# Weight differences of MoE 2 made during MoE 1, new planner durations, and routing ahead in VectorE's order

## The chip, the cores and the metric

One Trainium2 chip, of which the kernel uses one core. The time is device microseconds of one execution; three executions of the kernel before took 1979.09, 1979.22 and 1980.27 us (median 1979.22). All arithmetic is in 32-bit floats; matrix products are made from pairs of a rounded high part and a low part (three products instead of one).

## The reference

Three stages follow each other:

- Attention over a packed set: for 4 batches x 8 heads, 32 pack queries attend over 576 keys and values of 64 elements, and the 576 queries attend over the 32 results. Output: 2304 tokens x 512.
- MoE 1: h = x w_in (512 x 2048), g = h * clip(h + 3, 0, 6) / 6, y = g w_out (2048 x 512).
- MoE 2: a gate (512 x 8), exp of the logits, eight rounds in which P is divided by its row sums, then by its column sums, and scaled by N/E; then for each of 8 experts relu(x w1[e]) w2[e] with 1024 hidden columns, weighted by P[:, e] and summed.

## The kernel before

The 2304 tokens are 6 blocks of 384. Hidden columns are taken in groups of 256: MoE 1 has 8 groups, MoE 2 has 4 per expert, 32 in all.

The program isn't written in its final order. Operations are put into an `Order` with a duration for the planner (`t_dve`, `t_act`, `t_pool`, or a number), the buffers that they hold, their dependencies, a priority (a low number goes first) and a latency `lat` that followers have to wait. `Order.run` then picks operation after operation by earliest planned start and priority and so fixes each engine's instruction order. On the chip every engine runs its order strictly in sequence, with semaphore waits on true data dependencies; planned times have no other effect. `alt` gives an operation that POOL or DVE may take; a low part (`split_part`, L521) carries a surcharge `SPARE` of 1.0 on DVE. Operations with priorities from 100 up are planned with a small delay, `PATIENCE`.

MoE 1 runs 24 units (`units`; six blocks times four pairs of groups) of `layer1a` (L1017 to 1019) and `layer2a` (L1055 to 1057). Unit by unit, hidden values are rectified on ACT (L1030) and DVE (L1035) and split into a high part on ACT (L525) and a low part mostly on POOL (L530).

MoE 2 works on pairs of blocks with a Strassen-Winograd scheme of seven products in the first layer (`layer1b`, L1178 to 1180), evicted or added up by ACT (L412) and DVE (L1192). It has three passes over the 32 groups, one for each pair of blocks:

- In the first pass the weights are also prepared. Per group, `combined` loads w1 (512 KB, "raw"), makes the differences (`minus`, L552) and splits everything into the buffers w1 and w1x; `keep_first` stores them in memory (w1d). `plain_second` loads w2 and splits it. The first pass uses w2 as it is in `layer2b` (L1497 to 1499; accumulated on DVE, L1509 and L1521). For every two groups, a double unit, `keep_second` makes w2's differences for the later passes: four subtractions (T, L1271), four high parts on ACT (H, L1277), four low parts (T again, L1281), and stores the seven pairs into w2d.
- The second and third passes load w1 and w2 combinations ready made (`kept_first`, `kept_second`) and use seven products in the second layer too (`layer2s`, L1406 to 1408). Their inputs are made by `operands` (L1092 to 1107) at the beginning of a pass.

`by_turns` interleaves the products of one layer's generator with those that still wait from the unit before. `gate` and `routing` (L1583 to 1640) lie between MoE 1 and MoE 2; routing is one serial chain of small DVE instructions with one PE product with ones (L1627) per iteration, and `keep_shares` then transposes the shares (L1322, L1331) and stores them.

SBUF is reused by phases: `second_phase` closes attention's buffers and opens, among others, two buffers w1 and one w1x; `third_phase`, after MoE 1, opens T, H and a third raw buffer.

Of the kernel before, what the change touches and what calls it, by code (L numbers as in the profile page):

```python
# [62 lines left out]
MIXES = 0.5  # L63
D_PSUM, D_BOTH, D_SHARE, A_PSUM, A_SBUF, P_BOTH = 0.56, 0.8, 0.72, 0.5, 0.53, 1.2
# [83 lines left out]
def t_pool(n):  # L148
    return 0.15 + n / 465.0

# [6 lines left out]
def tile_kernel(  # L157
# [62 lines left out]
    def opened(tag, count):  # L220

        res[tag].free_at += [order.now] * count
# [27 lines left out]
    for tag in ("xy", "w1", "w1x", "w2s", "T", "H", "U", "PB"):  # L250
        places(tag, [])
    place("ph", ph, 2, 2)
    place("po", ph, 2, 2)
    late_tags = [(f"acc{j}", 1) for j in range(EARLY, NB)] + [("w1", 2), ("w1x", 1), ("tmp", 4)]
# [68 lines left out]
    order.now = 0.0  # L323
    places("raw", fixed(dp, "raw", 1024, 2))
# [158 lines left out]
    def raw_piece(src, prio, tag="raw"):  # L483

        c, n = src.shape[1], src.shape[2]
        r = hold(tag, [128, c * n], src.dtype)
        dma(
            512,
            lambda: nc.sync.dma_start(r.t.rearrange("p (c n) -> p c n", c=c), src),
            writes=[r], prio=prio,  # L490
        )
        return r
# [41 lines left out]
    def combined(g, prio):  # L534

        _, w1, _, f0 = groups[g]
        r = raw_piece(w1[:, f0:f0 + FG].rearrange("(c p) f -> p c f", p=128), prio)
        wa, wb = pair("w1", [128, 8, 128]), pair("w1x", [128, 6, 128])  # L540
        t1, t2, t3, t4 = (hold("m", [128, 2, 128]) for _ in range(4))
        raw = lambda: r.t.rearrange("p (c n) -> p c n", c=KC)
        b = {
            11: lambda: raw()[:, 0:2, 0:128],
            12: lambda: raw()[:, 0:2, 128:256],
            21: lambda: raw()[:, 2:4, 0:128],
            22: lambda: raw()[:, 2:4, 128:256],
        }

        def minus(o, i0, i1, deps, **kw):  # L550
            alt(
                t_dve(256), t_pool(256), lambda e: e.tensor_tensor(o.t, i0(), i1(), ALU.subtract),  # L552
                reads=deps, writes=[o], prio=prio, **kw,
            )
# [521 lines left out]
    def operands(pr, prio, after=lambda nth: ()):  # L1076
# [9 lines left out]
        def split(nm, c, src, held, deps):  # L1086
            dst = lambda x: o[nm].t[x][:, c, :]
            deps = [*deps, *turn[nm]]
            if c == 0:
                deps += begun[-1:]  # L1090
            high = act(
                t_act(TB), lambda: nc.scalar.activation(dst(0), src(), AF.Copy),  # L1092
                takes=[held], fills=[o[nm]], after=deps, prio=prio,
            )
            if c == 0:
# [3 lines left out]
                    t_dve(TB), t_pool(TB),  # L1099
# [5 lines left out]
        def mix(dst, i0, i1, how, deps, **kw):  # L1105
            return alt(
                t_dve(TB), t_pool(TB), lambda e: e.tensor_tensor(dst(), i0(), i1(), how),
                after=deps, prio=prio, **kw,
            )
# [27 lines left out]
    def rectified(quick, hs):  # L1137

        def finish(c, half, f, ps=None):
            src = (lambda: ps.t[:, :TB]) if ps else (lambda: c.t)  # L1140
            act(
                t_act(TB, bool(ps)), lambda: nc.scalar.activation(c.t, src(), AF.Relu),
# [95 lines left out]
    def plain_second(g, prio):  # L1238

        _, _, w2, f0 = groups[g]  # L1240
        r = raw_piece(w2[f0:f0 + FG, :].rearrange("(c p) d -> p c d", p=128), prio)
# [4 lines left out]
    def keep_second(k, ws, rs, prio):  # L1246
# [4 lines left out]
        t1, t2, t3, t4 = (hold("T", [128, NFC, n]) for _ in range(4))  # L1251

        def kept_at(nm, x):
            at = PLACE[nm] * 1024 + x * 512
            return W2D[k][:, at:at + 512]

        for nm, w, h in (("b11", ws[0], 0), ("b21", ws[1], 0), ("b22", ws[1], 1)):
            for x in range(2):
                store(
                    (2, k), 256, kept_at(nm, x).rearrange("p (c n) -> p c n", c=NFC),  # L1260
                    lambda w=w, h=h, x=x: w.t[x][:, :, h * n:(h + 1) * n], [w], prio,
                )
        for nm, t, i0, i1, deps in (
# [6 lines left out]
                t_dve(512), t_pool(512),  # L1270
# [3 lines left out]
        for nm, t in (("t1", t1), ("t3", t3), ("t2", t2), ("t4", t4)):  # L1274
            h = hold("H", [128, NFC, n], F32R)
            act(
                t_act(512), lambda t=t, h=h: nc.scalar.activation(h.t, t.t, AF.Copy), reads=[t], writes=[h], prio=prio,  # L1277
            )
            alt(
                t_dve(512), t_pool(512),  # L1280
# [3 lines left out]
            store((2, k), 256, kept_at(nm, 0).rearrange("p (c n) -> p c n", c=NFC), lambda h=h: h.t, [h], prio)  # L1284
            store(
                (2, k), 256, kept_at(nm, 1).rearrange("p (c n) -> p c n", c=NFC), lambda t=t: t.t, [t], prio
            )
# [28 lines left out]
    def keep_shares():  # L1316
# [8 lines left out]
            reads=[Pr], writes=[x], **kw,  # L1325
# [158 lines left out]
    def layer2b(i, g, blk, w2, hs):  # L1484
# [4 lines left out]
        for t in range(TB // 128):  # L1489
# [16 lines left out]
            elif e == 0:  # L1506
                last = dve(
                    t_dve(512),
# [9 lines left out]
            else:  # L1518
                last = dve(
                    t_dve(512),  # L1520
# [61 lines left out]
    def routing():  # L1582
        kw = dict(prio=41)  # L1583
        V = nc.vector
        m, mm, nm = once("mx", [128, 1]), once("mm", [1, 1]), once("nm", [128, 1])
        dve(t_dve(NTT * E), lambda: V.tensor_reduce(m.t, L.t, AX.X, ALU.max), reads=[L], writes=[m], **kw)
# [5 lines left out]
            reads=[ps], writes=[mm], **kw,  # L1592
# [13 lines left out]
        for it in range(8):  # L1606
            rs, cs, ct = once("rs", [128, NTT]), once("cs", [128, E]), once("ct", [128, E])
            ps = psum("ph")
            dve(t_dve(NTT * E), lambda rs=rs: V.tensor_reduce(rs.t, Pr.t, AX.X, ALU.add),
                reads=[Pr], writes=[rs], **kw)  # L1610
            dve(0.09, lambda rs=rs: V.tensor_scalar_add(rs.t, rs.t, 1e-9), writes=[rs], **kw)
            dve(0.15, lambda rs=rs: V.reciprocal(rs.t, rs.t), writes=[rs], **kw)
            dve(
                t_dve(NTT * E),
# [6 lines left out]
                t_dve(NTT * E),  # L1621
                lambda cs=cs: V.tensor_reduce(cs.t, Pr.t.rearrange("p t e -> p e t"), AX.X, ALU.add),
                reads=[Pr], writes=[cs], lat=1.5, **kw,
# [6 lines left out]
            dve(0.08, lambda ct=ct, ps=ps: V.tensor_scalar_add(ct.t, ps.t[:, :E], 1e-9),  # L1630
                reads=[ps], writes=[ct], **kw)
            dve(0.1, lambda ct=ct: V.reciprocal(ct.t, ct.t), writes=[ct], **kw)
            dve(0.08, lambda ct=ct: V.tensor_scalar_mul(ct.t, ct.t, float(NT) / float(E)), writes=[ct], **kw)
            dve(
                t_dve(NTT * E),
                lambda ct=ct: V.tensor_tensor(
                    Pr.t, Pr.t, ct.t[:, None, :].to_broadcast([128, NTT, E]), ALU.mult
# [16 lines left out]
    with tc.manual_schedule():  # L1654
# [37 lines left out]
        )  # L1692
        begun = len(order.all)
        for i, (blk, g) in enumerate(units):
# [23 lines left out]
        i = len(units)  # L1718
        turn = 100 + G1
        doubles = range((len(groups) - G1) // 2)  # L1720
# [3 lines left out]
        def by_turns(one, other):  # L1724

            for _ in one:
                next(other, None)

        done, preparing = [], []
        for d2 in doubles:  # L1730
# [18 lines left out]
            keep_second(d2, ws, rs, turn - 0.7)  # L1749
# [10 lines left out]
        for pr in range(1, NB // 2):  # L1760
            C = [hold(f"acc{2 * pr + h}", [128, KC, TB]) for h in range(2)]
            U = hold("U", [128, 2, TB])
            for d2 in doubles:
# [30 lines left out]
            if pr + 1 < NB // 2:  # L1794
                ops[pr + 1] = operands(pr + 1, 45, lambda n: [turns["hop"][-1]])
# [35 lines left out]
```

## Time and profile before

| | |
|---|---|
| median of 3 runs | 1979.22 us |
| profiled execution | 1980.84 us |
| its span | 1979.1 us |
| mean granted TensorE clock | 0.985 |
| PE busy | 1886.9 us, 95% |
| DVE, ACT, POOL busy | 77%, 44%, 55% |
| DMA queue q1 | 428 MB, 64.6% of 16 engines' span |

The span runs from the first to the last instruction. PE is TensorE's matmuls, PEld its weight loads, DVE VectorE, POOL GpSimd, SP the queue that issues the transfers. L numbers are lines of the kernel before. A wait is idle time of an engine just before an instruction, put down to what released it last. Attention fills the first 150 us or so, MoE 1 runs to about 460, the first pass of MoE 2 from there to about 1015, the second to about 1500 and the third to the end.

### The profile page before, as it was taken

To read this page: it belongs to the slowest core of one execution; us is meant where nothing else is said; L and a number is where in the kernel's file an instruction comes from. 1 tells how busy PE (TensorE), PEld (TensorE's weight loads), DVE (VectorE), ACT (ScalarE), POOL (GpSimd) and SP (SyncE) were. 2 spreads that over 40 slices of the span, in tenths; PEclk is the share of its full clock that TensorE was granted. 3 is DMA by queue.
4 is the path that set the end of the run, shared out by engine and by line. 5 is a ranking of instruction groups with operands and counts; after the bars stand their busy time and mean duration, and the time that the engine had idled before them with its cause. 6 is when DMAs were issued, how large, how long until landed. Compare 5 with 4: busy or idle time off the path is not lost.

```text
span 1979.1 us, 30944 instructions
## 1 busy us (share of the span) xinstructions
PE 1886.9 (95%) x11199; PEld 1784.3 (90%) x11199; DVE 1517.5 (77%) x2434; ACT 868.1 (44%) x1901; POOL 1088.6 (55%) x985
## 2 busy tenths in 40 slices
PE   6999999989899999999899999999998999999997
PEld 4889989987688888888789999999998999999997
DVE  6775574437988888888867887887787877877886
ACT  5764563435455555555543332333234332332332
POOL 3334473326766666666754655555465554554653
PEclk7999999999999999999999999999999999999999
DMA  9941122005677878787787777777776777777773
GB/s 204 195 99 37 51 75 81 12 17 174 256 270 282 296 250 310 259 310 261 256 294 257 262 255 253 265 260 259 256 262 219 263 263 256 260 262 253 262 247 96
DMA packets 189561, 430.19 MB, mean 217 GB/s; under 512 B 52305, under 2 KB 102625, under 8 KB 177121
## 3 DMA queue, kind: packets, MB, share of 16 engines
q1 hardware_dynamic: 189408, 428.23, 64.6%
q8 instruction: 88, 1.44, 0.3%
q14 instruction: 65, 0.52, 0.1%
HBM read 305.94 MB, written 122.23 MB: 216 GB/s over the span
## 4 chain that ended last, share of the span: by engine, by line
PE 71%; DVE 12%; DMA 6%; POOL 4%; issue 3%; ACT 3%; SPq 1%; POOLq 0%; DVEq 0%; ACTq 0%
PE ph L1178 9%; PE ph L1180 9%; PE ph L1179 9%; PE po L1408 8%; PE po L1407 8%; PE po L1406 8%; PE po L1055 3%; PE po L1057 3%; PE po L1056 3%; DMA raw<-in_moe_w_dram 2%; PE ph L1017 2%; PE po L1499 2%; PE po L1497 2%; PE po L1498 1%; PE ph L1019 1%
## 5 line engine op out<-in xcount | busy, mean ns | idle before, releaser
L530 POOL TENSOR_TENSOR hs<-tmp,hs 128x384 fp32r<-128x384 f32 x212 | 228.9, 1084 | 288.7 <-ACT hs L525 277.6
L1367 POOL TENSOR_TENSOR tmp<-tmp,tmp 128x384 f32<-128x384 f32 x127 | 131.2, 1033 | 347.3 <-DVE tmp L1155 344.9
L1354 ACT ACTIVATE xy<-tmp 128x384 fp32r<-128x384 f32 x296 | 147.2, 519 | 344.1 <-DVE tmp L1155 299.6
L1361 POOL TENSOR_TENSOR xy<-tmp,xy 128x384 fp32r<-128x384 f32 x209 | 252.8, 1223 | 45.4 <-ACT xy L1354 44.3
L1418 DVE TENSOR_TENSOR acc<-po,acc 128x384 f32<-128x384 f32 x304 | 166.9, 550 | 101.8 <-PE po L1408 101.5
L1192 DVE TENSOR_TENSOR tmp<-ph,tmp 128x384 f32<-128x384 f32 x288 | 158.6, 551 | 66.3 <-PE ph L1180 65.2
L1406 PE MATMUL po<-xy,w2s 128*128 128x384 f32 x592 | 198.9, 336 | 1.3 <-DVE U L1418 1.3
L1408 PE MATMUL po<-xy,w2s 128*128 128x384 f32 x592 | 199.6, 337 | 0.0
L1407 PE MATMUL po<-xy,w2s 128*128 128x384 f32 x592 | 199.6, 337 | 0.0
L412 ACT ACTIVATE tmp<-ph 128x384 f32<-128x384 f32 x281 | 135.9, 484 | 129.0 <-PE ph L1180 127.7
L1178 PE MATMUL ph<-ax,w 128*128 128x384 f32 x512 | 174.0, 340 | 3.2 <-ACT tmp L412 2.0
L1179 PE MATMUL ph<-ax,w 128*128 128x384 f32 x512 | 173.4, 339 | 0.6 <-POOL ax L1100 0.6
L1180 PE MATMUL ph<-ax,w 128*128 128x384 f32 x512 | 173.5, 339 | 0.0
L1155 DVE SCALAR_TENSOR_TENSOR tmp<-tmp,PB 128x384 f32<-128x384 f32 x192 | 153.3, 799 | 5.3
L1497 PE MATMUL po<-w,hs 128*128 128x512 f32 x384 | 152.1, 396 | 0.0
L1499 PE MATMUL po<-w,hs 128*128 128x512 f32 x384 | 151.5, 395 | 0.0
L1498 PE MATMUL po<-w,hs 128*128 128x512 f32 x384 | 150.5, 392 | 0.0
L1361 POOL TENSOR_TENSOR ax<-tmp,ax 128x384 fp32r<-128x384 f32 x110 | 134.6, 1236 | 21.2 <-ACT ax L1354 20.6
L1521 DVE SCALAR_TENSOR_TENSOR acc<-po,Pr,acc 128x512 f32<-128x512 f32 x168 | 123.8, 741 | 24.6 <-PE po L1499 24.5
L1354 ACT ACTIVATE ax<-tmp 128x384 fp32r<-128x384 f32 x152 | 76.7, 519 | 144.3 <-DVE tmp L1155 118.9
L1367 DVE TENSOR_TENSOR tmp<-tmp,tmp 128x384 f32<-128x384 f32 x129 | 132.1, 1042 | 1.1
L525 ACT ACTIVATE hs<-tmp 128x384 fp32r<-128x384 f32 x224 | 117.2, 523 | 23.4 <-DVE tmp L1035 11.8
(232 smaller groups left out, 5559.3 us busy)
## 6 DMA issues: line engine op xcount, KB each, us to landing
w2s<-w2d SPq DMA_DIRECT2D x224, 512.0 KB, 4.4
w<-w1d SPq DMA_DIRECT2D x64, 1024.0 KB, 6.3
w1x<-w1d SPq DMA_DIRECT2D x64, 768.0 KB, 5.8
raw<-in_moe_w_dram SPq DMA_DIRECT2D x64, 512.0 KB, 5.7
w1d<-w SPq DMA_DIRECT2D x32, 1024.0 KB, 5.0
w1d<-w1x SPq DMA_DIRECT2D x32, 768.0 KB, 5.5
w2d<-w SPq DMA_DIRECT2D x96, 256.0 KB, 3.3
w2d<-H SPq DMA_DIRECT2D x64, 256.0 KB, 4.2
```

What stands on the lines that cost most here:

```text
L530: lambda e: e.tensor_tensor(dst(w.t[1]), src(), as_f32(dst(w.t[0])), ALU.subtract),
L1178: nc.tensor.matmul(out, wh[:, at + c, :], bh[:, c, :], start=first and c == 0, **on)
L1179: nc.tensor.matmul(out, wh[:, at + c, :], bl[:, c, :], start=False, **on)
L1180: nc.tensor.matmul(out, wl[:, at + c, :], bh[:, c, :], start=False, **on)
L1354: A_SBUF, lambda: nc.scalar.activation(dst(0), t.t, AF.Copy),
L1361: lambda e: e.tensor_tensor(dst(1), t.t, as_f32(dst(0)), ALU.subtract),
L1367: D_BOTH, P_BOTH, lambda e: e.tensor_tensor(dst.t, i0.t, i1.t, how),
L1406: nc.tensor.matmul(o, wh[:, f, cs], ah[:, f, :], start=begin and f == 0, **on)
L1407: nc.tensor.matmul(o, wh[:, f, cs], al[:, f, :], start=False, **on)
L1408: nc.tensor.matmul(o, wl[:, f, cs], ah[:, f, :], start=False, **on)
L1497: nc.tensor.matmul(ps.t, hh[:, f, ts], wh[:, f, :], start=(f == 0), stop=False)
L1499: nc.tensor.matmul(ps.t, hl[:, f, ts], wh[:, f, :], start=False, stop=(f == NFC - 1))
```

## The change

1. `AHEAD` lists ten of the sixteen double units (0, 1, 2, 3, 5, 7, 9, 11, 13, 15). Their T work is taken out of the first pass: `keep_second` is cut into `keep_second` (the plain pieces) and `keep_differences`. During MoE 1's units 0 to 16 the two w2 matrices of such a double are loaded a second time, into "rawE", and `keep_differences` runs on buffers "TE" and "HE" with priority 101. These lie in the space of w1 and w1x, which MoE 2 gets only when all ahead operations are done (`first_weights`).
2. `plain_second` splits w2 in two halves of 512 columns instead of one operation of 1024.
3. Planner durations: `r_dve`, `r_pool` for the subtractions of `combined` and `keep_differences` and, after routing (`order.later`), for low parts; ACT conversions 0.1 more there; `D_BOTH`, `P_BOTH`, `A_SBUF`, `A_PSUM` in `operands` and `rectified`; 0.75 for the accumulations of `layer2b`.
4. Routing: priority 4 instead of 41 (evictions have 5), longer durations, `HAND` = 2.0 us of latency to PE instead of 1.5 or none, and the scaling by N/E folded into the multiplication that follows.
5. In the first double of the second pass the waiting `layer2b` products are taken at every second turn, and the buffers w2 and hs are given up one group later. The first two operands (a11, s3) of the third pass wait for an earlier point (`turns["hop"][-8]`).

```diff
+HAND = 2.0
+AHEAD_UNITS = 17
+AHEAD = (0, 1, 2, 3, 5, 7, 9, 11, 13, 15)
...
+def r_dve(n):
+    return 0.15 + n / 650.0
+def r_pool(n):
+    return 0.2 + n / 400.0
...
-    late_tags = [...] + [("w1", 2), ("w1x", 1), ("tmp", 4)]
+    late_tags = [...] + [("rawE", 2), ("TE", 4), ("HE", 3), ("tmp", 4)]
...
+        for tag, at, count, n in (("rawE", "w1_0", 2, 1024), ("TE", "w1_1", 4, 512), ("HE", "w1x0", 3, 512)):
+            t = late.tile([128, count * n], F32R if tag == "HE" else F32, tag=at, name=tag)
+            places(tag, quarters(t, n, count))
...
+    def first_weights():
+        opened("w1", 2)
+        opened("w1x", 1)
...
     def split_part(dst, src, w, n, deps, prio, **kw):
+        later = order.later
         high = act(
-            t_act(n), lambda: nc.scalar.activation(dst(w.t[0]), src(), AF.Copy),
+            t_act(n) + 0.1 * later, lambda: nc.scalar.activation(dst(w.t[0]), src(), AF.Copy),
...
-            t_dve(n), t_pool(n),
+            (r_dve if later else t_dve)(n), (r_pool if later else t_pool)(n),
...
     def plain_second(g, prio):
-        split_part(lambda d: d.rearrange("p c n -> p (c n)"), lambda: r.t, w, NFC * DM, [r], prio)
+        for c in range(NFC):
+            split_part(lambda d, c=c: d[:, c, :], lambda c=c: r.t[:, c * DM:(c + 1) * DM], w, DM, [r], prio)
...
     def routing():
-        kw = dict(prio=41)
+        kw = dict(prio=4)
...
-            dve(0.1, lambda ct=ct: V.reciprocal(ct.t, ct.t), writes=[ct], **kw)
-            dve(0.08, lambda ct=ct: V.tensor_scalar_mul(ct.t, ct.t, float(NT) / float(E)), writes=[ct], **kw)
+            dve(0.2, lambda ct=ct: V.reciprocal(ct.t, ct.t), writes=[ct], **kw)
             dve(
-                t_dve(NTT * E),
-                lambda ct=ct: V.tensor_tensor(
-                    Pr.t, Pr.t, ct.t[:, None, :].to_broadcast([128, NTT, E]), ALU.mult
+                0.6,
+                lambda ct=ct: V.scalar_tensor_tensor(
+                    Pr.t, Pr.t, float(NT) / float(E), ct.t[:, None, :].to_broadcast([128, NTT, E]), ALU.mult, ALU.mult
                 ),
...
+        doubles = range((len(groups) - G1) // 2)
+        ahead, todo = [], list(AHEAD)
         for i, (blk, g) in enumerate(units):
...
                 layer1a(i, blk, f, {b: pws[b, 2 * g + f // NFC] for b in batches}, hs[f // NFC])
+            if todo and len(AHEAD) * i >= (len(AHEAD) - len(todo)) * AHEAD_UNITS:
+                d2 = todo.pop(0)
+                at = len(order.all)
+                raws = [second_raw(G1 + 2 * d2 + n, 101, "rawE", turns["l1"]) for n in range(2)]
+                keep_differences(d2, raws, 101, "E")
+                ahead += order.all[at:]
+                if not todo:
+                    order.op([("", 0.0, first_weights)], after=ahead)
             layer2a(i, g, blk, [ws[2 * g][1], ws[2 * g + 1][1]], hs)
...
-            keep_second(d2, ws, rs, turn - 0.7)
+            keep_second(d2, ws, turn - 0.7)
+            if d2 not in AHEAD:
+                keep_differences(d2, rs, turn - 0.7)
...
-                    by_turns(layer1b(i, ops[pr], wa, wb, shared(prios(i)[1], pb, one_of)), waiting)
-                    if n == d2 == 0 and pr == 1:
+                    by_turns(layer1b(i, ops[pr], wa, wb, shared(prios(i)[1], pb, one_of)), waiting, 1 if behind or d2 else 2)
+                    if n and d2 == 0 and pr == 1:
...
-                ops[pr + 1] = operands(pr + 1, 45, lambda n: [turns["hop"][-1]])
+                ops[pr + 1] = operands(pr + 1, 45, lambda n: [turns["hop"][-8 if n < 2 else -1]])
```

## Rows read from the trace of the kernel before

**Rows 1.** The page: busy us by engine; granted TensorE clock in 40 slices.

```profile
PE 1886.9 (95%) x11199; PEld 1784.3 (90%) x11199; DVE 1517.5 (77%) x2434; ACT 868.1 (44%) x1901; POOL 1088.6 (55%) x985
...
PEclk7999999999999999999999999999999999999999
```

**Rows 2.** Windows: length, busy us by engine (x), granted clock, DMA share, GB/s.

```profile
150.00:390.00 240.00, 238.48 (x1735) 227.18 (x1738) 135.36 (x275) 119.28 (x276) 110.70 (x120) 1.00 0.16 53
390.00:475.00 85.00, 74.85 (x458) 66.19 (x451) 47.24 (x78) 36.20 (x79) 38.57 (x34) 0.96 0.16 53
475.00:570.00 95.00, 85.31 (x421) 75.29 (x420) 88.63 (x153) 51.78 (x109) 69.55 (x64) 0.98 0.69 249
570.00:990.00 420.00, 394.17 (x1928) 351.53 (x1927) 357.99 (x453) 233.38 (x496) 280.77 (x247) 0.98 0.80 280
990.00:1050.00 60.00, 55.52 (x284) 52.51 (x283) 40.58 (x55) 24.53 (x54) 28.96 (x26) 0.94 0.79 284
1050.00:1470.00 420.00, 420.00 (x2418) 420.00 (x2417) 336.32 (x516) 135.06 (x287) 230.27 (x201) 1.00 0.75 259
1470.00:1530.00 60.00, 52.19 (x297) 49.13 (x296) 51.77 (x71) 26.79 (x59) 41.99 (x36) 1.00 0.72 235
```

**Rows 3.** PE's waits, 570 to 990: releaser, us in total, times, longest.

```profile
PE ph L1178 <- DVE tmp L1192: 22.9, 12, 3.7
```

**Rows 4.** Source line L1497: ns min/median/max, first and last start.

```profile
L1497 PE MATMUL po<-w,hs x384: 387/391/632, 467.8 to 1015.4; 128*128 128x512 f32 x192
```

**Rows 5.** DVE in order of time, 766 to 781: start, us.

```profile
766.43 1.50 DVE L1271 TENSOR_TENSOR T<-raw,T 128x512 f32<-128x512 f32 x1
...
768.99 1.78 DVE L1281 TENSOR_TENSOR T<-T,H 128x512 fp32r<-128x512 f32 x1
...
774.85 2.37 DVE L1281 TENSOR_TENSOR T<-T,H 128x512 fp32r<-128x512 f32 x2
...
779.93 0.74 DVE L1521 SCALAR_TENSOR_TENSOR acc<-po,Pr,acc 128x512 f32<-128x512 f32 x1
780.59 0.54 DVE L1192 TENSOR_TENSOR tmp<-ph,tmp 128x384 f32<-128x384 f32 x1
```

**Rows 6.** Windows of L1271, then L1281: DVE busy, POOL busy, clock, DMA.

```profile
600.00:950.00 350.00, 26.87 (x22) 35.47 (x20) 0.99 0.81 283
600.00:950.00 350.00, 47.82 (x32) 18.22 (x12) 0.99 0.81 283
```

**Rows 7.** Source line L1281: ns min/median/max.

```profile
L1281 DVE TENSOR_TENSOR T<-T,H x38: 675/1776/1817, 468.5 to 978.7; 128x512 fp32r<-128x512 f32 x38
L1281 POOL TENSOR_TENSOR T<-T,H x26: 1272/1534/2125, 464.6 to 984.4; 128x512 fp32r<-128x512 f32 x26
```

**Rows 8.** The page, DMA issues: KB each, us to landing.

```profile
w2d<-H SPq DMA_DIRECT2D x64, 256.0 KB, 4.2
```

**Rows 9.** Groups by line, 150 to 390: busy us, mean ns, idle before.

```profile
L530 POOL TENSOR_TENSOR hs<-tmp,hs 128x384 fp32r<-128x384 f32 x67 | 69.2, 1044 | 99.9 <-ACT hs L525 96.9 <-issue 2.1 <-POOL w1f L456 0.5
...
L1035 DVE SCALAR_TENSOR_TENSOR tmp<-tmp,ph 128x384 f32<-128x384 f32 x68 | 37.3, 551 | 41.6 <-ACT tmp L1030 40.7
```

**Rows 10.** PE's waits, 475 to 570.

```profile
PE ph L1627 <- DVE cs L1622: 6.5, 4, 2.8
PE ph L1331 <- DVE tmp L1322: 3.0, 1, 3.0
```

**Rows 11.** Group of L1633, 475 to 570.

```profile
L1633 DVE TENSOR_SCALAR ct<-ct 128x8 f32<-128x8 f32 x8 | 4.9, 618 | 0.3
```

**Rows 12.** PE's waits, 990 to 1050.

```profile
PE ph L1178 <- DMA w<-w1d: 4.5, 1, 4.5
```

**Rows 13.** PE's waits, 1470 to 1530.

```profile
PE ph L1179 <- DVE xy L1100: 1.6, 2, 1.4
...
PE ph L1179 <- DVE ax L1100: 0.8, 1, 0.8
PE ph L1179 <- POOL xy L1100: 0.7, 1, 0.7
```

More of the change, by code (lines that the diff above doesn't have):

```diff
@@ L249, in tile_kernel @@
     BLK = KC // 2 * TB * 2
-    for tag in ("xy", "w1", "w1x", "w2s", "T", "H", "U", "PB"):
+    for tag in ("xy", "w1", "w1x", "w2s", "T", "H", "U", "PB", "rawE", "TE", "HE"):
         places(tag, [])
@@ L253, in tile_kernel @@
     place("po", ph, 2, 2)
-    late_tags = [(f"acc{j}", 1) for j in range(EARLY, NB)] + [("w1", 2), ("w1x", 1), ("tmp", 4)]
+    late_tags = [(f"acc{j}", 1) for j in range(EARLY, NB)] + [("rawE", 2), ("TE", 4), ("HE", 3), ("tmp", 4)]
     def second_phase():
@@ L323, in tile_kernel @@
     order.now = 0.0
+    order.later = False
     places("raw", fixed(dp, "raw", 1024, 2))
@@ L481, in split_f64, with raw_piece @@
             join(lambda: at(w.t).bitcast(U32), reads=[m, t], fills=[w])
-    def raw_piece(src, prio, tag="raw"):
+    def raw_piece(src, prio, tag="raw", after=()):
         c, n = src.shape[1], src.shape[2]
@@ L489, in raw_piece @@
             lambda: nc.sync.dma_start(r.t.rearrange("p (c n) -> p c n", c=c), src),
-            writes=[r], prio=prio,
+            writes=[r], prio=prio, after=after,
         )
@@ L1238, in plain_second, with second_at, keep_second, keep_differences @@
     def plain_second(g, prio):
-        _, _, w2, f0 = groups[g]
-        r = raw_piece(w2[f0:f0 + FG, :].rearrange("(c p) d -> p c d", p=128), prio)
+        r = second_raw(g, prio)
         w = pair("w2", [128, NFC, DM])
-        split_part(lambda d: d.rearrange("p c n -> p (c n)"), lambda: r.t, w, NFC * DM, [r], prio)
+        for c in range(NFC):
+            split_part(lambda d, c=c: d[:, c, :], lambda c=c: r.t[:, c * DM:(c + 1) * DM], w, DM, [r], prio)
         return w, r
-    def keep_second(k, ws, rs, prio):
+    def second_at(k, nm, x):
+        at = PLACE[nm] * 1024 + x * 512
+        return W2D[k][:, at:at + 512].rearrange("p (c n) -> p c n", c=NFC)
+    def keep_second(k, ws, prio):
+        n = DM // 2
+        for nm, w, h in (("b11", ws[0], 0), ("b21", ws[1], 0), ("b22", ws[1], 1)):
+            for x in range(2):
+                store(
+                    (2, k), 256, second_at(k, nm, x),
+                    lambda w=w, h=h, x=x: w.t[x][:, :, h * n:(h + 1) * n], [w], prio,
+                )
+    def keep_differences(k, rs, prio, tag=""):
         n = DM // 2
@@ L1250, in keep_second @@
         b11, b12, b21, b22 = raws
[L1251 to L1262, printed above, removed]
+        t1, t2, t3, t4 = (hold("T" + tag, [128, NFC, n]) for _ in range(4))
         for nm, t, i0, i1, deps in (
@@ L1274, in keep_second @@
         for nm, t in (("t1", t1), ("t3", t3), ("t2", t2), ("t4", t4)):
-            h = hold("H", [128, NFC, n], F32R)
+            h = hold("H" + tag, [128, NFC, n], F32R)
             act(
-                t_act(512), lambda t=t, h=h: nc.scalar.activation(h.t, t.t, AF.Copy), reads=[t], writes=[h], prio=prio,
+                t_act(512) + 0.1, lambda t=t, h=h: nc.scalar.activation(h.t, t.t, AF.Copy),
+                reads=[t], writes=[h], prio=prio,
             )
             alt(
-                t_dve(512), t_pool(512),
+                r_dve(512), r_pool(512),
                 lambda e, t=t, h=h: e.tensor_tensor(t.t.bitcast(F32R), t.t, as_f32(h.t), ALU.subtract),
@@ L1283, in keep_second, with second_raw @@
             )
[L1284 to L1287, printed above, removed]
+            store((2, k), 256, second_at(k, nm, 0), lambda h=h: h.t, [h], prio)
+            store((2, k), 256, second_at(k, nm, 1), lambda t=t: t.t, [t], prio)
+    def second_raw(g, prio, tag="raw", after=()):
+        _, _, w2, f0 = groups[g]
+        return raw_piece(w2[f0:f0 + FG, :].rearrange("(c p) d -> p c d", p=128), prio, tag, after)
     def kept_first(g, prio):
@@ L1324, in keep_shares @@
             ),
-            reads=[Pr], writes=[x], **kw,
+            reads=[Pr], writes=[x], lat=HAND, **kw,
         )
@@ L1519, in layer2b @@
                 last = dve(
-                    t_dve(512),
+                    0.75,
                     lambda row=row, share=share, ps=ps: nc.vector.scalar_tensor_tensor(
@@ L1582, in routing @@
     def routing():
-        kw = dict(prio=41)
+        kw = dict(prio=4)
         V = nc.vector
         m, mm, nm = once("mx", [128, 1]), once("mm", [1, 1]), once("nm", [128, 1])
-        dve(t_dve(NTT * E), lambda: V.tensor_reduce(m.t, L.t, AX.X, ALU.max), reads=[L], writes=[m], **kw)
+        dve(t_dve(NTT * E), lambda: V.tensor_reduce(m.t, L.t, AX.X, ALU.max), reads=[L], writes=[m], lat=HAND, **kw)
         ps = psum("ph")
@@ L1591, in routing @@
             lambda ps=ps: V.tensor_reduce(mm.t, ps.t[:1, :128], AX.X, ALU.max, negate=True),
-            reads=[ps], writes=[mm], **kw,
+            reads=[ps], writes=[mm], lat=HAND, **kw,
         )
@@ L1608, in routing @@
             ps = psum("ph")
-            dve(t_dve(NTT * E), lambda rs=rs: V.tensor_reduce(rs.t, Pr.t, AX.X, ALU.add),
+            dve(0.3, lambda rs=rs: V.tensor_reduce(rs.t, Pr.t, AX.X, ALU.add),
                 reads=[Pr], writes=[rs], **kw)
-            dve(0.09, lambda rs=rs: V.tensor_scalar_add(rs.t, rs.t, 1e-9), writes=[rs], **kw)
-            dve(0.15, lambda rs=rs: V.reciprocal(rs.t, rs.t), writes=[rs], **kw)
+            dve(0.2, lambda rs=rs: V.tensor_scalar_add(rs.t, rs.t, 1e-9), writes=[rs], **kw)
+            dve(0.25, lambda rs=rs: V.reciprocal(rs.t, rs.t), writes=[rs], **kw)
             dve(
-                t_dve(NTT * E),
+                0.6,
                 lambda rs=rs: V.tensor_tensor(
@@ L1620, in routing @@
             dve(
-                t_dve(NTT * E),
+                0.4,
                 lambda cs=cs: V.tensor_reduce(cs.t, Pr.t.rearrange("p t e -> p e t"), AX.X, ALU.add),
-                reads=[Pr], writes=[cs], lat=1.5, **kw,
+                reads=[Pr], writes=[cs], lat=HAND, **kw,
             )
@@ L1718, in tile_kernel, with by_turns @@
         i = len(units)
+        order.later = True
         turn = 100 + G1
-        doubles = range((len(groups) - G1) // 2)
         begun = len(order.all)
         waiting = iter(())
-        def by_turns(one, other):
-            for _ in one:
-                next(other, None)
+        def by_turns(one, other, each=1):
+            for n, _ in enumerate(one):
+                if n % each == 0:
+                    next(other, None)
         done, preparing = [], []
```

18 lines of the change are left out of this document (9 added, 9 removed).

## Prediction

> **What bounds the kernel now.** I read the page first: PE is busy 95% of the span, and PEclk shows the full level in all slices but the first [rows 1] (a digit hides what is under a tenth). An average of 95% hides stages with different limits, so the second view is busy time by stage, with boundaries set where the lines of MoE 1, of the first pass and of the kept-weight passes begin [rows 2]. The reader is to see four things in it. In 1050 to 1470 PE has no idle time at full clock: nothing that is moved can help there. In 150 to 390 (MoE 1) PE idles 240 - 238.5 = 1.5 us, while DVE works 56%, POOL 46% of the time and the DMA engines 16%: this stage has room on the engines that are not its bound. In 570 to 990 (the first pass of MoE 2, in which every unit's weights are also prepared) PE idles 420 - 394.2 = 25.8 us and loses 2% of 420, 8.4 us, to the lower clock level of 1.2 GHz: 34.2 us. The seams lose too: 390 to 475, 10.2 + 3.4 = 13.6; 475 to 570 (the routing lies here), 9.7 + 1.9 = 11.6; 990 to 1050, 4.5 + 3.6 = 8.1; 1470 to 1530, 7.8. All of it is 75 us, and the change can't give back more, since it takes no large product away.
>
> Who makes PE wait in the first pass is the third view. Nearly all of its idle time there ends with DVE's addition out of PSUM at L1192, 12 waits of up to 3.7 us [rows 3]: one in every double unit (32 units, 16 doubles, from 467.8 to 1015.4, so 34 us each [rows 4]). The fourth view, DVE's instructions in order of time before one of these waits, tells why DVE is late [rows 5]: from 766.4 to 779.9 it runs almost without a break, and inside stand one T difference (L1271, 1.50 us) and three low parts of T (L1281, 1.78 and 2.37 us), 5.65 us in all. The addition that PE waits for starts at 780.59, behind them. So the first pass is a PE stage that DVE, in its fixed order, trips once per double.
>
> **The T work and what it costs.** A double unit's differences are 4 subtractions (L1271), 4 high parts on ACT and 4 low parts (L1281), 8 stores of 256 KB. From 600 to 950 there are 22 + 20 of L1271 [rows 6], so 10.5 doubles of 33.3 us each; L1271 and L1281 take 26.9 + 47.8 = 74.7 us of DVE, 7.1 per double, and 35.5 + 18.2 = 53.7 of POOL, 5.1 per double. One such operation has no fixed price: on DVE the low part takes 0.675 at least and 1.776 in the median, on POOL 1.272 at least and 2.125 at most [rows 7]. It is long where the other engine works too.
>
> **Part 1, ten of sixteen doubles made during MoE 1.** Removed from the first pass: 10 x (7.1 DVE + 5.1 POOL), and their stores (8 of 256 KB, 4.2 us to landing each [rows 8]). DVE's 358 busy of 420 [rows 2] is 28.4 per 33.3 us; a relieved double needs 21.3 of PE's 30.6 (420 - 34.2, over 12.6 doubles), so DVE need not be late in it. Doubles 0 to 3 are all relieved, from 4 on every second one, so that an unrelieved one has a relieved neighbour to catch up in. Loss now 34.2/12.6 doubles = 2.7 each. I take 0.4 for a relieved one (6.5 of them in this stretch: half of 3, and 5 to 15) and 1.7 for each of the other 6, which keep their T work, but whose w2 is split in halves (one conversion and one subtraction more per unit, in exchange for shorter blocks in DVE's order) and is planned with longer costs: 2.6 + 10.2 = 12.8, a gain of 21. Ends: 0, if something else trips PE once per double, and 32, if the stretch becomes like 1050 to 1470.
>
> Added to MoE 1: per double 2 loads of 512 KB (the first pass reads these matrices again), the same 8 operations, 4 conversions, 8 stores. Their buffers open when attention's are closed (about 150) and the last is asked for in unit 16 of 0 to 23. MoE 1 makes 68/4 = 17 units in 240 us, 14.1 each [rows 9], so with 7 units left before 467.8 the last one begins near 355: some 200 us for ten. At first-pass durations they add 71 to DVE's 113 and 51 to POOL's 92 in that time, 92% and 72%; at the least durations, split half and half, 4 x 0.675 and 4 x 1.272 per double, they add 27 and 51. Both fit, the first barely. What is behind a late operation: POOL's low part of hs, which waits 96.9 us for ACT now and so has slack [rows 9], and DVE's evictions, with four PSUM banks for each layer. Price: between 0 (as 1050 to 1470 runs, with DVE at 80% and PE never idle) and the first pass's own loss rate, 34.2/420 x 200 = 16. I take 5, nearer to the first because MoE 1's DVE work is still mostly from PSUM. The transfers go into SP's queue at 0.16 of the engines' time; 31 MB more over 200 us, at the 259 GB/s for 0.75 of 1050 to 1470, make that near 0.6, under the 0.75 at which 1050 to 1470 runs without idle PE. What a store that waits there for a late T holds back are MoE 1's weight loads for later units and the first weights of MoE 2.
>
> The SBUF page of the Trainium skill (SBUF — State Buffer, Who interferes with whom) has it that a DVE instruction with two SBUF inputs and a GpSimd one hold one pair of ports in turn, each for its whole length. [Rows 7] agree: 0.675 + 1.27 is about what the long ones take. By that rule ten doubles need 10 x 7.3 = 73 us of the port at the least durations, beside POOL's 92: 165 of 200, so it would still fit.
>
> **Part 2, routing first.** In 475 to 570 PE's idle time is 6.5 for the column sums and 3.0 for the transposes of the shares [rows 10], both behind DVE: PE's order has the routing matmuls at planned times that DVE doesn't meet. Put first in DVE's order, with 2.0 us of planned hand-over instead of 1.5 and one instruction less per iteration (8 x 0.618 = 4.9 us of DVE [rows 11]), they come in time. DVE there is busy 88.6 of 95, and loses the T work of four doubles as well, so evictions that now stand behind routing (1 to 2 us at a time) are taken in by the banks. Gain 7 of the 11.6 (0 to 11).
>
> **Part 3, seams.** The second pass's first units take layer2b's products at half the rate and give up hs later. PE's one wait in 990 to 1050 is 4.5 for kept weights [rows 12]; at half the rate two more products, of some 1.4 us each (6 matmuls), lie between the release of that w1 buffer and its next use, and the clock that is lost around the wait (3.6) may stay up: gain 4 (0 to 8). The third pass's a11 and s3 are made one double earlier; PE's waits for ACT, DVE and POOL operands in 1470 to 1530 [rows 13] hold 1.6 + 0.8 + 0.7 = 3.1 for such splits: gain 4 (-3 to 5, since the splits then stand among a full double's work). 390 to 475: first weights are now made after the ahead work, from about 355 on, where DVE and POOL are half free; 0 (-5 to 5). Other planner costs move no work by themselves; 0.
>
> **Sum.** 21 - 5 + 7 + 4 + 4 = 31. The profiled execution took 1980.8 with a span of 1979.1; the median of the runs is 1979.2, so spans can be read as times, and 1979.2 - 31 = 1948.
>
> **Rivals.**
> 1. MoE 1 becomes the tripped stage. For it: at first-pass durations DVE reaches 92% there, above the 85% at which the first pass loses. Against: 68 of MoE 1's evictions have one SBUF input and run at 0.551 us [rows 9], not stretched. It pays 16, the unrelieved doubles gain nothing (first pass 6.5 x 2.3 = 15 less): 1979 - 15 + 16 - 7 - 8 = 1965.
> 2. The change doesn't do what it says: the once-per-double wait is not the T work's but that of the splits and combinations that fill the rest of the block. For it: 766.4 to 779.9 is 13.5 us, and only 5.65 of it are T work [rows 5]. Against: PE's waits are 22.9/12 = 1.9 us on average [rows 3], less than that. The first pass gives 4, routing and seams 15, MoE 1 costs 5: 1965.
> 3. Slower. The two w1 buffers and w1x are opened to MoE 2's weights only when the last ahead operation is done; before the change nothing of MoE 1 holds them. If ahead work runs late to the end of MoE 1 (from about 450 on it decides), PE faces the preparation of the first groups with nothing to run: one group is half a double, 17 us, two 34, plus MoE 1's 16, against 36 of gains: 1979 - 36 + 34 + 16 = 1993. Against it: some 100 us lie between the last double's planned begin and 467.8.
> 4. Better: unrelieved doubles are freed as well, routing and seams give nearly all they can, and MoE 1 pays nothing: 1979 - 30 - 11 - 9 = 1929.
>
> **How the numbers follow.** Forecast (1938 to 1959) 0.58; rival 1, 0.13; rival 2, 0.10; rival 3, 0.07; rival 4, 0.08; near no change 0.04. A measurement of this kernel tells 0.2%, 4 us, from no change. Faster 0.89, same 0.04, slower 0.07. The range leaves out rival 3, the case of no change and, of rival 4, what goes beyond it (0.03), 0.14 in all: 1924 to 1975.
>
> **What would show it.** Right: L1271 and L1281 have 80 of their 128 instructions between 150 and 380; DVE falls to about 75% in the first pass, and the waits of PE for L1192 halve in number, those left in unrelieved doubles; no PE wait for L1622 over 1 us; PE idle in 150 to 390 stays under 7 us. Wrong: PE idle over 10 us in MoE 1, a wait of PE for w1 or its splits after 460, or as many waits for L1192 as before.

## The result

The changed kernel takes 1932.48 us (median of 4 runs, 1931.4 to 1936.19) against 1979.74 before: a ratio of 0.9761, 95% interval 0.9744 to 0.9779, 47 us. The forecast was 1948 (1924 to 1975), a gain of 31. In the experiments most of the gain came from another edit than the one that the forecast credited.

In the page after, busy time of PE (two lines of the page: busy us by engine, granted clock) stands beside [rows 1]:

```profile
PE 1871.9 (97%) x11199; PEld 1776.3 (92%) x11199; DVE 1476.1 (76%) x2401; ACT 879.3 (46%) x1929; POOL 1158.5 (60%) x1046
...
PEclk7999999999999999999999999999999999999999
```

DVE works 41 us less than before, POOL 70 us more. Busy time by stage, as in [rows 2] but with boundaries that suit both kernels (window, length, PE, PEld, DVE, ACT, POOL busy, clock, DMA share, GB/s):

```profile
150.00:400.00 250.00, 239.93 (x1705) 225.43 (x1704) 186.48 (x320) 140.23 (x314) 168.35 (x154) 0.98 0.51 174
400.00:485.00 85.00, 78.47 (x487) 69.78 (x486) 43.31 (x73) 35.01 (x77) 36.67 (x37) 0.98 0.13 47
485.00:585.00 100.00, 97.36 (x497) 87.74 (x496) 80.37 (x150) 54.80 (x120) 67.39 (x68) 1.00 0.62 218
585.00:950.00 365.00, 365.00 (x1835) 329.73 (x1834) 285.90 (x383) 219.96 (x473) 284.09 (x261) 1.00 0.76 268
950.00:1040.00 90.00, 88.97 (x490) 85.66 (x489) 65.25 (x96) 35.68 (x77) 49.17 (x42) 1.00 0.84 291
```

The kernel before in the three stretches that the experiments speak of most:

```profile
150.00:400.00 250.00, 246.86 (x1782) 234.45 (x1782) 144.93 (x290) 125.94 (x290) 118.05 (x127) 1.00 0.15 50
485.00:585.00 100.00, 90.31 (x446) 79.77 (x445) 92.09 (x149) 52.52 (x111) 73.24 (x65) 0.98 0.72 257
585.00:950.00 365.00, 343.76 (x1688) 306.91 (x1688) 314.01 (x397) 204.05 (x434) 244.41 (x220) 0.99 0.81 282
```

From 585 to 950 PE has no idle time any more (21.2 before), in relieved and in unrelieved doubles alike, with DVE at 78%. In 150 to 400 it idles 10.1 us instead of 3.1, and 2% of the stretch, 5 us, goes to the lower clock level of 1.2 GHz: MoE 1 pays.

Milestones give the same in one sum, since the work of each stretch is nearly the same. Three source lines mark them (ns min/median/max, first and last start): MoE 1's second layer by its last start, the second pass's second layer and the transposes of the output by their first. Before:

```profile
L1055 PE MATMUL po<-hs,w2oh x192: 335/338/338, 70.1 to 459.5; 128*128 128x384 f32 x192
...
L1406 PE MATMUL po<-ax,w2s x304: 332/336/522, 1031.2 to 1953.7; 128*128 128x384 f32 x152
...
L1466 PE MATMUL po<-ident,acc x48: 271/272/329, 1504.8 to 1969.8; 128*128 128x128 f32 x48
```

and after:

```profile
L1076 PE MATMUL po<-hs,w2oh x192: 335/338/522, 69.8 to 471.9; 128*128 128x384 f32 x192
...
L1435 PE MATMUL po<-ax,w2s x304: 332/336/446, 989.4 to 1911.4; 128*128 128x384 f32 x152
...
L1495 PE MATMUL po<-ident,acc x48: 271/272/328, 1456.9 to 1921.8; 128*128 128x128 f32 x48
```

MoE 1 ends 471.9 - 459.5 = 12.4 us later. From there to the second pass's first second-layer product it is 517.5 instead of 571.7, 54.2 less; from there to the first transposes 6.1 less; the third pass is the same. 12.4 - 54.2 - 6.1 = -47.9.

What PE still waits for, in a part of MoE 1 and around the routing (PE's waits in 250 to 330, then in 490 to 600: us, times, longest):

```profile
PE ph L979 <- DVE tmp L1056: 4.6, 2, 4.2
PE po L1077 <- POOL hs L551: 1.6, 2, 1.4
...
PE po L1526 <- DVE acc L1550: 2.6, 1, 2.6
```

None of [rows 3], [rows 10] or [rows 12] is left: L1213 (the former L1192), the column sums and the kept weights keep PE waiting no more.

### The profile page after: what moved, and what is told of

It reads as the page before. It is cut to its first block, busy times and chain, and to the rows that moved or that the text cites. A ratio compares the mean times of both kernels' runs of the same rounds, so it can differ in the third digit from the quotient of the medians.

```text
span 1931.0 us, 30998 instructions
## 1 busy us (share of the span) xinstructions
PE 1871.9 (97%) x11199; PEld 1776.3 (92%) x11199; DVE 1476.1 (76%) x2401; ACT 879.3 (46%) x1929; POOL 1158.5 (60%) x1046
## 4 chain that ended last, share of the span: by engine, by line
PE 84%; DVE 7%; DMA 3%; ACT 3%; POOL 2%; issue 1%; SPq 0%; POOLq 0%; ACTq 0%; DVEq 0%
PE ph L1199 12%; PE ph L1201 12%; PE ph L1200 12%; PE po L1437 8%; PE po L1436 8%; PE po L1435 8%; PE po L1526 5%; PE po L1528 5%; PE po L1527 4%; PE po L1077 2%; PE po L1076 2%; PE po L1078 2%; PE ph L1038 1%; DMA raw<-in_moe_w_in_dram 1%; PE ph L1040 1%
## 5 line engine op out<-in xcount | busy, mean ns | idle before, releaser
L1213 DVE TENSOR_TENSOR tmp<-ph,tmp 128x384 f32<-128x384 f32 x288 | 159.1, 553 | 73.2 <-PE ph L1201 72.0
L1199 PE MATMUL ph<-ax,w 128*128 128x384 f32 x576 | 193.5, 336 | 1.5 <-DVE tmp L1056 1.5
L1201 PE MATMUL ph<-ax,w 128*128 128x384 f32 x576 | 193.5, 336 | 0.0
L1200 PE MATMUL ph<-ax,w 128*128 128x384 f32 x576 | 193.2, 335 | 0.0
L1550 DVE SCALAR_TENSOR_TENSOR acc<-po,Pr,acc 128x512 f32<-128x512 f32 x168 | 124.8, 745 | 61.3 <-PE po L1528 61.2
L1176 DVE SCALAR_TENSOR_TENSOR tmp<-tmp,PB 128x384 f32<-128x384 f32 x192 | 149.1, 777 | 5.2
L1199 PE MATMUL ph<-xy,w1x 128*128 128x384 f32 x384 | 129.0, 336 | 1.4 <-ACT tmp L432 1.4
```

Source lines behind the costliest of these rows:

```text
L1199: nc.tensor.matmul(out, wh[:, at + c, :], bh[:, c, :], start=first and c == 0, **on)
L1200: nc.tensor.matmul(out, wh[:, at + c, :], bl[:, c, :], start=False, **on)
L1201: nc.tensor.matmul(out, wl[:, at + c, :], bh[:, c, :], start=False, **on)
```

## The experiments

Each was timed beside the kernel before (medians 1980.6 to 1980.8), so ratios can be compared; where two intervals overlap, the difference is not clear of the noise. Windows and waits are of one execution of each kernel.

**Ahead work taken away, and ahead work alone.** These two undo and isolate the edit that the forecast put first.

```diff
-AHEAD = (0, 1, 2, 3, 5, 7, 9, 11, 13, 15)
+AHEAD = ()
...
+        first_weights()
```

> The changed kernel with no double made ahead: all sixteen doubles' T work in the first pass, every other edit kept. Theory (the T work on DVE is what tripped the first pass): the first pass loses 20 to 30 us again, MoE 1 gets its 12 us back, 1942 to 1952 in all. Rival (the longer planned durations and the shorter splits freed the first pass): the first pass stays without idle PE and MoE 1 gets faster, 1920 us, under the changed kernel's 1932.

> The kernel before with the ten doubles made ahead as the one edit; planner durations, w2's split, routing and seams as before. Theory (T work): first pass gains 20 to 25, MoE 1 pays 12, about 1968. Rival (durations): nothing gained in the first pass, MoE 1 pays, 1985 to 1992.

Without ahead work: 1925.95 us, ratio 0.9727 (0.9713 to 0.9742): not slower but faster than the changed kernel's 0.9761, nearer to the rival than to the theory. Ahead work alone: 1979.47, ratio 0.9995 (0.9986 to 1.0005): nothing, between its two expectations. So the T work need not leave the first pass. In the kernel without ahead work all of it is there; these are its subtractions, then its low parts, from 600 to 950 (columns as in [rows 6]):

```profile
600.00:950.00 350.00, 52.04 (x43) 1.29 (x1) 1.00 0.84 298
600.00:950.00 350.00, 16.42 (x12) 46.18 (x31) 1.00 0.84 298
```

DVE runs 43 + 12 = 55 of these operations, in the kernel before 22 + 32 = 54 [rows 6]. All work of this kernel, 585 to 950 (columns as in the table by stage):

```profile
585.00:950.00 365.00, 363.43 (x1820) 326.68 (x1819) 319.99 (x394) 230.74 (x493) 322.19 (x290) 1.00 0.83 297
```

DVE and POOL are both busy 88% of the time there, more than in the kernel before (314 and 244 of 365), and PE idles 1.6 us. A busy share near 90% is not by itself what makes PE wait. Ahead work alone shows the reverse, in MoE 1 and in the first pass:

```profile
150.00:400.00 250.00, 235.53 (x1678) 222.00 (x1677) 185.66 (x320) 139.79 (x313) 161.03 (x147) 0.97 0.51 174
485.00:585.00 100.00, 97.75 (x493) 87.12 (x494) 79.96 (x155) 55.21 (x116) 66.27 (x67) 1.00 0.65 224
585.00:950.00 365.00, 347.63 (x1700) 306.36 (x1698) 272.24 (x366) 195.86 (x411) 224.34 (x197) 0.99 0.71 247
```

DVE is down to 272 of 365, and PE still idles 17.4 us (before 21.2). Who waits there (PE's waits, then DVE's and POOL's):

```profile
PE ph L1199 <- DVE tmp L1213: 8.8, 5, 2.7
PE ph L1199 <- ACT tmp L432: 5.1, 6, 1.6
PE po L1527 <- DVE hs L551: 2.8, 4, 0.8
...
DVE ms L573 <- DMA raw<-in_moe_w_dram: 69.0, 21, 6.2
...
POOL ms L573 <- DVE ms L573: 60.0, 21, 5.2
```

The DVE time that was freed turned into 69.0 us of waiting: DVE stands at the first difference of a newly loaded w1 (L573), whose load hasn't landed, and PSUM additions and POOL's own differences stand behind it. The kernel before doesn't lose its time in this way: there DVE waits 7.1 us for these loads, as much as in the changed kernel, and works almost without a break ahead of the addition that PE waits for [rows 5] (DVE's waits from 585 to 950, before, then after):

```profile
DVE ms L552 <- DMA raw<-in_moe_w_dram: 7.1, 8, 1.2
```

```profile
DVE ms L573 <- DMA raw<-in_moe_w_dram: 7.1, 8, 1.5
```

So under the old plan one loss took the place of another. Ahead work did help where DVE was truly full, around the routing (485 to 585: idle 2.3 instead of 9.7), and after the end of MoE 1 it gave 20 us altogether (551.7 to the second pass's first second-layer product, where the kernel before has 571.7); but MoE 1 ended 19.2 us later, which takes nearly all of it back.

**What the planner believes.** The old durations put back, all of them, and in two parts:

```diff
-                r_dve(512), r_pool(512),
+                t_dve(512), t_pool(512),
...
-                    0.75,
+                    t_dve(512),
...
-        order.later = True
```

> The changed kernel with the short planned durations of before outside routing (subtractions, low and high parts, operands, layer2b's accumulations); ahead work, w2 in halves, new routing and seams kept. Theory by now (the first pass was tripped by an instruction order planned with too short durations): PE's waits for L1192's and L412's successors come back in 600 to 950, 12 to 25 us slower than the changed kernel, 1945 to 1958. Rival (the halves of w2 did it): 1930 to 1936.

> The changed kernel with the short planned durations of before for layer2b's accumulations, operands and the rectified first pass; splits and subtractions keep the long ones. If the accumulations' (0.60 planned, 0.74 measured, three in every half unit) are what tripped the first pass: 1950 to 1965. If the splits' are: 1932 to 1938.

> The changed kernel with the short planned durations of before for splits and subtractions (low parts, high parts, differences); accumulations and operands keep the long ones. If the splits' are what tripped the first pass: 1950 to 1965. If the accumulations' are: 1932 to 1940.

With all short durations back 1968.69 us, ratio 0.9941 (0.9923 to 0.9958), 36 us slower than the changed kernel and beyond what was expected: 24 of them lie between MoE 1's end and the second pass's second layer (541.8 instead of 517.5), the rest mostly in MoE 1, which ends 10.5 later (482.4) and whose ahead work is planned with the same durations. With the accumulations' alone it is 1937.57 (0.9781, 0.9752 to 0.9809), 5 slower, with intervals that overlap; with those of splits and subtractions alone 1958.98 (0.9892, 0.9863 to 0.9921), 26.5 slower. The waits are back, on the same engines (PE's, then DVE's, all durations short):

```profile
PE ph L1199 <- DVE tmp L1213: 10.8, 10, 2.6
PE ph L1199 <- ACT tmp L432: 4.0, 4, 1.7
...
DVE ms L573 <- DMA raw<-in_moe_w_dram: 67.2, 17, 5.5
```

Is it DVE's load? Not by these figures: with all short durations back, DVE is busy less than in the changed kernel (264 us instead of 286, and 0.75 instead of 0.78 us for each us of PE's work), and PE idles 14.9 us instead of none:

```profile
585.00:950.00 365.00, 350.06 (x1725) 309.88 (x1724) 264.23 (x374) 202.92 (x444) 248.53 (x228) 1.00 0.72 251
```

With the short durations of splits and subtractions alone, PE waits for L1213 six times in this stretch, some 65 us apart, each time just behind the T work of one of the six doubles that keep it; and DVE has no break ahead of the addition, as in [rows 5] (PE's waits from 585 to 950, then DVE in order of time before the wait that ends at 746.6):

```profile
PE ph L1199 <- DVE tmp L1213: 12.0, 6, 2.5
...
741.30 2.38 DVE L1307 TENSOR_TENSOR T<-T,H 128x512 fp32r<-128x512 f32 x2
743.61 0.74 DVE L1550 SCALAR_TENSOR_TENSOR acc<-po,Pr,acc 128x512 f32<-128x512 f32 x1
744.27 0.67 DVE L1307 TENSOR_TENSOR T<-T,H 128x512 fp32r<-128x512 f32 x1
744.87 0.55 DVE L1213 TENSOR_TENSOR tmp<-ph,tmp 128x384 f32<-128x384 f32 x1
```

So T work does trip PE where the plan has it at 0.60 us (0.675 to 1.8 measured [rows 7]), and hardly does where the plan has it at 0.94.

The durations alone, on the kernel before:

> The kernel before with the new planned durations outside routing as the one edit: no ahead work, w2 in one piece, routing and seams as before. Theory (the durations carry the gain, ahead work alone gave 1979.5): 1943 to 1952, which is the no-ahead kernel with old routing (1936) plus the seams' 11. Rival (durations help only together with ahead work or the seams): 1965 to 1980.

1946.37 us, ratio 0.9819 (0.9785 to 0.9853): 34 of the 47 us. From 585 to 950 PE idles 3.2 us instead of 21.2, with DVE busy about as long as before (310 of 365, while PE does 5% more). DVE's waits for loads are a sixth of those under ahead work alone, but not fewer than the 7.1 us of the kernel before:

```profile
585.00:950.00 365.00, 361.76 (x1806) 324.12 (x1806) 310.48 (x394) 221.68 (x462) 293.14 (x262) 1.00 0.82 296
```

```profile
DVE ms L574 <- DMA raw<-in_moe_w_dram: 11.2, 9, 3.9
```

The durations in the plan moved work, too. The kernel before gave 38 of 64 low parts of T to DVE [rows 7]; the changed kernel, in the first pass, 6 of 24 (source line). T's subtractions went the other way, as the kernel without ahead work shows above.

```profile
L1307 POOL TENSOR_TENSOR T<-T,H x18: 1287/1502/1758, 601.2 to 913.1; 128x512 fp32r<-128x512 f32 x18
L1307 DVE TENSOR_TENSOR T<-T,H x6: 1109/1466/1822, 601.2 to 912.5; 128x512 fp32r<-128x512 f32 x6
```

DVE's total load isn't what trips PE, then; but which engine an operation goes to and where it stands in the queue change together in these runs, and which of the two does it, they don't part. w2's halves, which could also do it, do nothing that shows: in one piece again, 1934.15, ratio 0.9765 (0.9735 to 0.9795).

```diff
-        for c in range(NFC):
-            split_part(lambda d, c=c: d[:, c, :], lambda c=c: r.t[:, c * DM:(c + 1) * DM], w, DM, [r], prio)
+        split_part(lambda d: d.rearrange("p c n -> p (c n)"), lambda: r.t, w, NFC * DM, [r], prio)
```

> The changed kernel with w2 split in one operation of 1024 columns again. Theory (durations): 1932 to 1937. Rival (shorter blocks in DVE's order did it): 1945 to 1958.

**Routing and seams.**

```diff
     def routing():
-        kw = dict(prio=4)
+        kw = dict(prio=41)
```

> The changed kernel with routing as before (priority 41, short planned durations, hand-over 1.5, one instruction more per iteration). Theory (PE waited for column sums that DVE made late): 6 to 10 us of waits come back, 1939 to 1943. Rival (DVE is relieved by the missing T work, so that routing comes in time in any order): 1932 to 1934.

> The changed kernel without ahead work and with routing as before: durations, w2's halves and the seams alone. Theory (ahead work costs in MoE 1 what it gives, and routing first with longer planned steps makes the chain end later): 1920 to 1924, the fastest so far. Rival (the T work of the first doubles, the routing chain and the evictions meet on DVE between 485 and 585 and need either edit): 1930 to 1938.

(The first also has the old durations, hand-over and instruction in routing, the second no ahead work besides.) Old routing in the changed kernel: 1928.87, ratio 0.9740 (0.9725 to 0.9755): 3.6 faster, with intervals that overlap, and in any case not slower. Without ahead work: 1936.07, ratio 0.9775 (0.9749 to 0.9800), where new routing had 1925.95: 10 slower. The first expectation missed on both sides; the second came out as its rival had it; and what one edit gives depends on the other. Durations, w2's halves and seams alone, the second of these kernels, gain 44.7 of the 47 us. The chain of eight iterations, by PE's column sums, in the changed kernel and with old routing:

```profile
L1656 PE MATMUL ph<-cs,ones x16: 170/214/256, 489.6 to 549.6; 128*128 128x8 f32 x16
```

```profile
L1656 PE MATMUL ph<-cs,ones x16: 170/214/256, 480.0 to 528.2; 128*128 128x8 f32 x16
```

Routing first takes 60 us, routing last 48, perhaps because the longer hand-over and steps in the plan spread the chain (priority, durations and hand-over weren't tried apart), and one PSUM addition that needs the shares keeps PE waiting 2.6 us (L1550, above); with old routing PE waits for nothing from 490 to 950. That holds while four doubles' T work is out of DVE's way. With it there, PE waits 4.1 + 2.0 for old routing's products:

```profile
PE ph L1361 <- DVE tmp L1352: 4.1, 1, 4.1
PE ph L1657 <- DVE cs L1652: 2.0, 2, 1.4
```

But new routing without ahead work waits as long there, for the addition that needs the shares (PE's waits from 485 to 585):

```profile
PE po L1527 <- DVE acc L1551: 6.1, 1, 6.1
```

So the 10 us between these two don't come from the routing's own stretch. With old routing 7.4 us are lost from 585 to 950, with new routing 1.6, and DVE waits 34.0 us there for loads instead of 10.8; why the plan behind routing comes out worse wasn't tried. The seams:

```diff
-                    by_turns(..., waiting, 1 if behind or d2 else 2)
-                    if n and d2 == 0 and pr == 1:
+                    by_turns(..., waiting)
+                    if n == d2 == 0 and pr == 1:
...
-                ops[pr + 1] = operands(pr + 1, 45, lambda n: [turns["hop"][-8 if n < 2 else -1]])
+                ops[pr + 1] = operands(pr + 1, 45, lambda n: [turns["hop"][-1]])
```

> The changed kernel with both seams as before (products taken at every turn, w2 and hs given up as before, the third pass's a11 and s3 not earlier). Theory (the seams give what the milestones of the two traces show between the end of the first pass and the third): 8 to 16 us slower, 1941 to 1948. Rival (the seams' waits are gone with the first pass's late DVE): 1932 to 1935.

1943.70, ratio 0.9818 (0.9802 to 0.9834), 11.2 slower. The waits of before are there again, or others of the same kind, and the clock over 950 to 1040 is 0.96 where the changed kernel has 1.00 (PE's waits in 950 to 1040, then in 1420 to 1540):

```profile
PE ph L1199 <- DMA w<-w1d: 4.0, 1, 4.0
...
PE ph L1200 <- POOL ax L1121: 2.4, 2, 1.7
...
PE ph L1199 <- ACT ax L1113: 1.0, 1, 1.0
```

**MoE 1's price, and less of it.** If durations planned too short cost 34 us, they may be what MoE 1 pays too. The first kernel below has longer ones for the decoding of the weights, the rectifier and the accumulations of MoE 1, and sets `order.later` before MoE 1's units:

```diff
-        fast = t_dve(n, True)
+        real = tag == "m"
+        fast = 0.42 if real else t_dve(n, True)
...
-            t_act(TB, True) + 0.1,
+            0.58,
...
-            t_dve(TB),
+            D_PSUM,
...
+        order.later = True
```

The second differs from the first in `AHEAD`, and also, which its expectation doesn't name, in longer durations of `out_of`, where a weight product of MoE 1 is split out of PSUM:

```diff
-AHEAD = (0, 1, 2, 3, 5, 7, 9, 11, 13, 15)
+AHEAD = (0, 1, 2, 3)
...
-                t_act(n, True), lambda: nc.scalar.activation(dst(0), src(), AF.Copy),
+                t_act(n, True) + 0.1, lambda: nc.scalar.activation(dst(0), src(), AF.Copy),
...
-                t_dve(n),
+                t_dve(n) + 0.08,
```

> The changed kernel with routing as before and, in MoE 1 too, planned durations near the measured ones (decoding, rectifying, splitting, accumulating). Theory (MoE 1 pays for the ahead work because its order is planned too short, not because an engine is full): idle time of PE in 150 to 400 falls from 9 to under 4 us, 1919 to 1924 against 1929 for the changed kernel with old routing. Rival (DVE and POOL are simply too full there, or stretch each other): 1927 to 1931.

> The fastest kernel so far (routing as before, planned durations near the measured ones in MoE 1 too; 1919) with the first four doubles made ahead instead of ten. Theory (ahead work pays only for the doubles that meet routing between 485 and 585; the others cost MoE 1 what it loses and the first pass runs full with its T work anyway): idle PE in 150 to 400 falls from 7 to about 3, 485 to 585 and 585 to 950 stay within 2 us of full, 1913 to 1918. Rival (the first pass needs more relief): 585 to 950 loses 4 to 8 us as in the kernel without ahead work and with old routing, 1920 to 1926.

Longer durations in MoE 1, with old routing: 1919.14 us, ratio 0.9696 (0.9667 to 0.9724), 9.7 under the same kernel with short ones and in the range expected. Idle time from 150 to 400 fell to 7.3, with no clock loss, and not under 4: so part of the price is the plan's, part the work's. With four doubles ahead instead of ten and `out_of` longer it is 2.7, and the time 1907.54 us, ratio 0.9634 (0.9606 to 0.9663), the fastest of all, less than the 1913 to 1918 expected and 25 us under the changed kernel. What it gains on the first lies in MoE 1, which ends at 447.9 instead of 459.8; from there to the second pass's first second-layer product both take 515 us. How much of it is due to `out_of` wasn't tried. The two kernels' windows:

```profile
150.00:400.00 250.00, 242.73 (x1741) 228.19 (x1741) 192.08 (x323) 142.59 (x320) 172.95 (x158) 1.00 0.52 176
```

```profile
150.00:400.00 250.00, 247.35 (x1810) 235.14 (x1809) 169.38 (x304) 131.62 (x301) 142.15 (x140) 1.00 0.29 98
485.00:585.00 100.00, 99.89 (x507) 90.03 (x506) 81.78 (x136) 59.33 (x131) 74.89 (x73) 1.00 0.69 243
585.00:950.00 365.00, 363.98 (x1830) 328.71 (x1829) 320.08 (x393) 225.75 (x482) 316.72 (x284) 1.00 0.85 303
950.00:1040.00 90.00, 90.00 (x515) 89.23 (x514) 70.69 (x105) 34.02 (x73) 52.51 (x45) 1.00 0.81 286
```

Twelve doubles' T work is back in the first pass, DVE is busy 320 of 365, and PE idles 1.0. DVE hardly waits for loads:

```profile
DVE ms L574 <- DMA raw<-in_moe_w_dram: 3.4, 6, 0.7
```

## Why the prediction was right, and where it was wrong

- "So the first pass is a PE stage that DVE, in its fixed order, trips once per double": this holds for the order of before. With the short durations of splits and subtractions back, PE trips six times, in the six doubles that keep their T work. But I took the operations ahead of L1192 in [rows 5] for load that has to go. DVE at 86% with the old plan idles PE 21 us, DVE at 88% with the new one and as many T operations 1.6: it is the plan that puts them ahead of an addition that PE needs.
- "Other planner costs move no work by themselves; 0": this is the step that failed, a term put at nothing. The durations are worth 34 us alone (durations alone against before). They move work between DVE and POOL in both directions and change what stands ahead of what in DVE's queue. Less load on DVE isn't the reason, and fewer waits for loads neither, as the kernel before had only 7.1 us of them; which change in the order does it stays open.
- "2.6 + 10.2 = 12.8, a gain of 21" for ahead work in 570 to 990: ahead work alone takes 3.9 us of idle time from 585 to 950, since DVE then stands at loads. Rival 2's price of 4 for the first pass is what ahead work alone gives, though not for its reason, the other splits and combinations; and another edit of the change freed the stage.
- MoE 1, "I take 5": 12.4 in the changed kernel, 19.2 with ahead work alone, inside the bounds of 0 and 16 only for the first. PE's 10.1 us of idle time there is a sign that the prediction had named as wrong; of the signs of being right, the waits for L1192 went altogether, and DVE fell to 78%.
- Routing, "gain 7": PE's waits in [rows 10] went, as forecast, but routing first is not what they need: with ahead work, old routing shows none of them either and is no slower. The evictions behind routing, which I let the banks take in, cost 2.6, and 6.1 without ahead work.
- Seams, "4" and "4": 11.2 together. The clock around the 4.5 us wait came back with it, as said.
- The sum had the sign and, with 31 for 47, most of the size because the stage's loss was read right (34.2 in [rows 2], next to nothing left of it); the edit that removes it was misnamed. That is luck in part: 21 of the 31 were put on ten doubles that alone gain nothing, and an edit put at 0 took their place. The 1932.48 measured lies outside the 1938 to 1959 held likeliest, nearest to rival 4's 1929; of its conditions the unrelieved doubles were freed, but MoE 1 did pay.

## What to carry to other kernels

Where engine orders are fixed by a planner, measure its durations on the chip, with the neighbours working, before moving work: 34 of 47 us came from better numbers, and ten moved doubles alone gained nothing. An engine that is late is not shown to be full: look at what it waits for itself, and whether it got less busy without the waits going. Move work ahead only for the stretch where the engine really has no time left, here probably four doubles around the routing (no kernel with MoE 1's longer durations and no double ahead was run), and check what the stage that takes it pays.

## What was not expected of the hardware

DVE and POOL could both be busy 88% of a stretch while PE ran at full clock with 0.4% idle time; beforehand 86% and 67% went with 6%. MoE 1, with DVE at 75% and POOL at 67% from 150 to 400, lost 4% of PE's time and some clock: fill alone tells neither.
